# Nine halved token blocks instead of four plain ones and eight halved ones, in an order that the planner chooses itself

## The chip, the cores and the metric

The kernel runs on one core of a Trainium2 chip. The metric is the device time of one execution in microseconds (us); lower is better. Two runs of the kernel before took 1121.74 and 1127.53 us, a median of 1124.63 us.

## The reference

```python
# attention: q, k, v are (8, 8, 576, 64), omega is (128, 64)
scale = 1.0 / np.sqrt(np.sqrt(D)); q_s, k_s = q * scale, k * scale
def phi(x):
    h = np.einsum('bhsd,md->bhsm', x, omega) - np.sum(x * x, -1, keepdims=True) / 2.0
    return np.exp(h - np.max(h, axis=-1, keepdims=True)) / np.sqrt(m)
q_p, k_p = phi(q_s), phi(k_s)
kv = np.einsum('bhsm,bhsd->bhmd', k_p, v); z = np.sum(k_p, axis=2)
attn = np.einsum('bhsm,bhmd->bhsd', q_p, kv) / (np.einsum('bhsm,bhm->bhs', q_p, z)[..., None] + 1e-06)
x = attn.transpose(0, 2, 1, 3).reshape(8, 576, 512)
# Fourier mixing, normalisation, two dense layers
mixed = np.real(np.fft.fft(np.fft.fft(x, axis=1), axis=2))
u = x + mixed
un = (u - mean(u)) / np.sqrt(var(u) + 1e-06)            # over the last axis
out = u + np.maximum(un @ w_ch1, 0.0) @ w_ch2           # w_ch1 (512, 2048), w_ch2 (2048, 512)
```

All matrix work is done in float32. The two weight matrices arrive as float64 and are narrowed to float32 on the chip.

## The kernel before

The 8 x 576 = 4608 rows pass through two parts.

**The first part** holds the attention, the Fourier mixing and the preparation of the weights. `attn` runs 32 times, once for each pair of heads: transposes on TensorE (PE, L607), projections (L701), a row maximum on VectorE (DVE, L644), exponentials on ScalarE (ACT, L661), the products with v and with the features (L735, L782, L790), and a division (L799 to L811). Four pairs make one batch, and `mix` runs once for each of the 8 batches: `folds` adds and subtracts halves on DVE or GpSimd (POOL) (L838 to L874), PE multiplies with sine and cosine tables (L894, L904, L944, and L955 for the middle column), and `residual` joins the cosine part, the sine part and the middle column on DVE (L993, L996) and adds the result to x (L1005, L1006). The sums u go to the tensor `us` in DRAM. `narrow` turns each 512-column piece of the float64 weights into float32 (L532 to L550), first w1, then w2; `w2_parts` makes the sums of w2 that the second part needs (L1484) and stores them in `w2l`.

**The dense layers** work on tokens in two ways. Plain rows are multiplied as they stand: `plain_of` takes 128 rows at a time, with 64 first-layer products (L1236), 16 second-layer products 512 columns wide (L1259), a relu between them (`hidden`, L1220 and L1222) and `rest`. Halved blocks of 512 rows use Strassen's scheme in Winograd's form: one layer of a block is 7 outer products of half-size matrices instead of 8 (`first_of` for the first layer, `product_of` for the second), and most outer products are split again into 7 "leaves" of 4 small products each (`leaf`: L1727 first layer, L2178 second layer). An outer product that is not split again runs at L1878; `single(j)` names those. Before the change the first 512 rows are plain (`NPLAIN = 4`), and the other 4096 rows are 8 halved blocks: block 0 with six of its seven first-layer products unsplit, block 1 alone ("narrow", 128-column leaves), and blocks 2 to 7 in three pairs ("wide", first-layer leaves 256 columns wide; `WIDE = 2`). The plain rows are multiplied in the first part, between the attention's own products; the halved blocks make up the second part. The attention's PE work, the plain rows and the second part follow one another on the same PE queue.

**The order.** Every stream of work (a generator) yields `Step`s with an engine, an expected cost, events to wait for, and buffers and PSUM banks to take and give back. `Listing.run` merges the streams into one in-order list per engine. Left to itself it takes at each turn the step that can begin first by its own clock (`FIRST`, `SECOND`), and of those within a small slack the one with the earliest due time. Where a step may run on DVE or POOL, it takes the one that would finish first. Before the change this choice is overridden: the strings `PICKS` and `PICKS2` name the stream and the engine of each step, `BANKS` and `BANKS2` the PSUM bank, and `BETWEEN` and `BETWEEN2` the places at which the norms of blocks 1 to 3 (`ahead`, L1596 to L1610) are slipped in, in buffers borrowed from the attention.

**Names that the steps below touch.** `w1_sums` makes the outer sums of w1 (`so5`, `so6`, `so3`) that the outer products 5, 6 and 3 multiply with; `sums_right` makes the token sums `tt`; `wl` are the tiles into which the 49 second-layer leaves of w2 are loaded for each narrow block or pair; `tag_of` says which buffer such a tile takes; `wash` are a few short matmuls at the seam of the two parts.

Of the kernel before, what the change touches and what calls it, by code (L numbers as in the profile page):

```python
# [33 lines left out]
NL = 2  # L34
# [7 lines left out]
class Clock(NamedTuple):  # L42
# [23 lines left out]


PICKS = (
    "40e0fff03eafdaege3OcdceefdcOdeccfgda37ghj0gjj7hlP79aj7ik97i8S7efhjffeHldffiehdjfdOihgihidaKedbhhciff"
    "ecgOfeejdfdPdeeedgifdffdefd8aiii88jhd8jP8b99i8e8jcddghjgheiifcOcdciieicgPgdefJcdghbkededfgcRbggb79ij"  # L70
    "8hi7hjafN9Haj9gfffeg8eif8hcej1jccc7ehidbhffLigebfbe6766gggfcbjahj9Ofghhjj8dQkkgT6jghff8de6dUjfhbgegh"
    "cefhafjUf8jgciSjOckkhjakkaeikggjlioklnhSgodoXON7l7l6nnj9icadc97cibf98ejH88a7edhMlhkmjjaQVijihkkfplSm"
    "okliljjilVaghVhnmljkmpjkhhnmkimlgglmbjpjjQ9d9alafhhdjlaMdjback0j766k7lh4g896ck6gkki77gij5ijhgj6dimni"
    "3ndjgi6Kc4jldlKikbkaijLhf75dcjlmklk36ci45jciekajkkkk5kihokeaeoLaioNlencidonbSiljjcmjjkboijTUUhgcfkik"
    "hiflkmeFF99nol5m8jT7naabda89Rbj97ecdl8cjilOgifkQb4acahg57ebbgabgdjkdTkk6eceebb5f9dg4R6ce486ggg6egfhh"
    "fg4g9egf5cbdhgPRhhcgjhggejigibLmHnbedijj6NOb7biihi9bgihMkaffPa8cijdhbdghbaeibNefffacjicigifi99975ih5"
    "jgj8699ajfg6g7fgefd65bO6Kalkkgd5jgjikagfldliPJpeoaeeefgdejadgilgScljiii5e65k56kl57k7j67S9lilk9gliih6"
    "ffkgec4fg4dbgg7fedaiP5gfbheefilddddddeghg9kbfncgghcfkkafkagGngb65p5Hopoj4bhoanbelli68bjjl5b7dlhighhi"
    "lflhpkgiWomjknmmmkimnjbjhn9jkmFKkfFgedccff6Wf7idUVhi8Th3fogbqp8fgmkeSdjna7ckenoghmnmffnjeo79q6547oa4"
    "nlkpd7aceonnc8blSVicilbhmjim8fh7SnnIl5mUkfjgfhhfhihg8ghfbS4kjf83j4lllb79jei8mnkblfnmmiolpilOUi9Mh5l5"  # L80
    "pmnaem79jjVmkbblek5iji9a9kffTgjikhiShfgjafhgfigh4g50PPP0ba5Pdh9dghdK77hgfdcbg8OO988jMehefibjjkellfcc"
    "PcdhQMihfQcffbKCf82b3c98cbcdcd6a299efgddbJaGQQbefLa9ecf74gg986HRgf9idg8kQeheff7be6ff2e5cc8fbcgdKP8f8"
    "9hN9Lc999bddcHcNb7Oc9effegd7ibhQeQ8haf7ccghhlUikhHW5lWmm5dkMQGM71fS6d1gdb99747ifddhIfdhhdhfdbihgiljn"
    "gWgijgg93ekKl8kEhIIbT3jjKgkb9k9eTfhkhlje34m49974iG66h68faHe6e7a79982975aI94a39c8cM8b4aa7ab984fge8eLM"
    "98b86ce8PbFPc9cbe6cKPf3a9b94fIdIQeJKbd876eJPdc5fNb7ffbf9JSS8RiLa4a7gPbajfgg8gdfhg2i2787Hf6OcdIN5d3LH"
    "accd46ddeKK72dJc7bbaa4bb9a9bc7c0777dghhdf7Bfddebd76ff1fddIe9949438686bc6aca85348dHcG7a5be957b55d1544"
    "9Gc1F5a9a68446344584584E59189970955888574443113301110"
)

BANKS = (  # L90
    "0102346120164024306243643016204164024320632462014021604606245062345042604670426420340267407231640260"
    "4524016460620240674206206415704602546064320143607264506402346234062732017426042106147026740260462462"
    "0410652604632452017205467402624060404256174302642060245016745202642016420634520520650162505605260250"
    "1675602501605204672016204567627450264102316742067460260462045642062637230724672402630145420640106240"
    "5264023026731602454230412046450416725730620424670121726154305610207453"
)

PLACES = "kkktttkktuuu"  # L100


BETWEEN = (
    "1684016841169001690116950169501695016950171011710117101175011750217502175031762417625176361766317664"
    "1769217692176931769417712177121776317774177751785317853179041790417926180471804818055180551806618066"
    "1814518145182071820718207182081820818208182261822618377183881846718468"
)


BETWEEN2 = (  # L110
    "006390119901259015590198902149023690236a0262a0265a0301a0329a0355a0426a0486b0528b0528b0550b0552b0563b"
    "0578b"
)

PICKS2 = (
    "020022020000018019023022023020020024021020025024019125125023025023023023028044023022020017018042042043"
    "026040041018018018018035120041034040035034120041043042048023032046030045045037044037046019120120040031"
    "040119019031022036038030032032024045145045145049033122047036034039017047033042042048023046037045025036"
    "043027042019024141143042119045038036048032049033022025050050039036039041043048031034044043022028049044"
    "023054033018032040039053047048027031018039037053038028052053036050040043040048054049038053053036047020"  # L120
    "046037048044117126039023032043042037024044026035044037043032051024025054019046046038119033053047052044"
    "035028044048028041049047047147019044042046044119046044046044048050040053031038025037038039033025052019"
    "046038047135041035029150048034131148033044044050147053028040025144142043147030046047021045043047029042"
    "029053045039052046045051029038038052050026037050049050046046049047051049041044151040040048043050049032"
# [1509 lines left out]

# [754 lines left out]
```

## Time and profile before

| what | value |
|---|---|
| two runs, median | 1121.74 and 1127.53, 1124.63 us |
| span of the profiled execution (first to last instruction) | 1119.2 us |
| PE busy | 1108.4 us (99%) |
| DVE busy | 888.7 us (79%) |
| ACT busy | 539.5 us (48%) |
| POOL busy | 390.6 us (35%) |
| mean granted TensorE clock | 0.999 |
| last plain product begins (L1259) | 416.5 us |
| last row maximum of the attention begins (L644) | 355.3 us |

The profile is of one execution, for which the span is given and no time of its own; the span lies 2.5 us below the faster of the two timed runs and 5.4 us below their median. A float32 product appears in the trace as two PE instructions. The windows view gives for each stretch of the span the busy time of each engine, with the number of instructions in brackets, the granted clock (1.00 is full), the share of the DMA engines and GB/s.

### The profile page before, as it was taken

The numbers are of one execution on the slowest core, as the hardware profiler recorded it, in microseconds if no ns is written. First come the engines' busy times: TensorE is split into PE (matmuls) and PEld (weight loads), VectorE is DVE, ScalarE is ACT, GpSimd is POOL, SyncE is SP. The second block draws the span as 40 slices with busy tenths as digits, with TensorE's granted clock in tenths as the row PEclk, the third lists the DMA queues.
The fourth block names the chain that finished last, engine by engine and source line by source line (L and its number), as shares of the span: only waits on it lengthen the run. The fifth ranks groups of instructions, "written<-read, shape, count | busy, mean of one in ns | idle before, by whom it ended". The sixth has DMA issues, their size and how long they took to land.

```text
span 1119.2 us, 31666 instructions
## 1 busy us (share of the span) xinstructions
PE 1108.4 (99%) x12467; PEld 1000.4 (89%) x12467; DVE 888.7 (79%) x1685; ACT 539.5 (48%) x1644; POOL 390.6 (35%) x401
## 2 busy tenths in 40 slices
PE   9999999999999999999999999999999999999998
PEld 7888888879868778999999889999889999889998
DVE  6999999987576767687697777888677888568895
ACT  7998898856536455623214452223463223331221
POOL 2443443553563348634413464000365000152000
PEclk9999999999999999999999999999999999999999
DMA  8856766665674669798896778747678656546453
GB/s 243 243 174 188 242 180 191 183 208 176 216 232 156 194 172 343 224 314 262 260 326 224 226 216 248 207 148 238 206 207 261 207 155 216 170 152 220 146 160 105
DMA packets 196549, 236.13 MB, mean 211 GB/s; under 512 B 53808, under 2 KB 120624, under 8 KB 196400
## 3 DMA queue, kind: packets, MB, share of 16 engines
q1 hardware_dynamic: 195904, 233.83, 68.1%
q8 instruction: 99, 1.62, 0.6%
q14 instruction: 50, 0.41, 0.1%
q10 hardware_dynamic: 496, 0.26, 0.1%
HBM read 182.13 MB, written 56.10 MB: 213 GB/s over the span
## 4 chain that ended last, share of the span: by engine, by line
PE 92%; DVE 3%; ACT 2%; DMA 2%; issue 0%; POOL 0%; SPq 0%; DVEq 0%; ACTq 0%
PE banks L2178 31%; PE banks L1727 27%; PE banks L1236 5%; PE banks L701 5%; PE banks L607 5%; PE banks L1259 5%; PE banks L1878 4%; PE banks L735 3%; PE banks L782 2%; PE banks L944 2%; PE banks L894 1%; ACT e L661 1%; DVE nmx L644 1%; PE banks L904 1%; DMA unw<-turned 1%; DMA raw<-in_moe_w_ch_dram 1%
## 5 line engine op out<-in xcount | busy, mean ns | idle before, releaser
L2178 PE MATMUL banks<-wl,sums 128*128 128x128 f32 x1792 | 219.8, 275 | 0.0
L2178 PEld LDWEIGHTS banks<-wl,sums 128*128 128x128 f32 x1792 | 210.6, 192 | 1.0 <-issue 0.3
L661 ACT ACTIVATE e<-banks,nmx 128x128 f32<-128x128 f32 x576 | 165.7, 441 | 23.3 <-DVE nmx L644 22.9
L644 DVE TENSOR_REDUCE nmx<-banks 128x8 f32<-128x1024 f32 (+1 forms) x96 | 89.3, 951 | 16.8 <-PE banks L701 12.4
L2178 PE MATMUL banks<-wl,hid 128*128 128x128 f32 x768 | 99.2, 275 | 0.3 <-DVE part L2154 0.3
L2178 PEld LDWEIGHTS banks<-wl,hid 128*128 128x128 f32 x768 | 92.8, 192 | 1.2 <-DVE part L2154 0.8
L2149 ACT ACTIVATE s<-banks 128x128 f32<-128x128 f32 x112 | 30.9, 277 | 113.6 <-PE banks L2178 103.5
L1727 PE MATMUL banks<-unw,wxw 128*128 128x256 f32 x352 | 85.4, 379 | 0.0
L701 PE MATMUL banks<-om,kqT 64*64 64x128 f32 (+1 forms) x2088 | 79.0, 275 | 1.7 <-ACT kv L751 1.3
L701 PEld LDWEIGHTS banks<-om,kqT 64*64 64x64 f32 (+1 forms) x2088 | 64.5, 138 | 12.7 <-issue 3.2
L2178 PE MATMUL banks<-wl,hx 128*128 128x128 f32 x576 | 74.2, 275 | 0.4 <-DVE part L2154 0.4
L1727 PEld LDWEIGHTS banks<-unw,wxw 128*128 128x128 f32 x352 | 66.6, 190 | 8.9
L1727 PE MATMUL banks<-rx,wxw 128*128 128x256 f32 x288 | 70.8, 379 | 0.0
L2178 PEld LDWEIGHTS banks<-wl,hx 128*128 128x128 f32 x576 | 69.4, 192 | 0.8 <-DVE part L2154 0.6
L1752 ACT ACTIVATE s<-banks 128x512 f32<-128x512 f32 x65 | 38.5, 596 | 65.1 <-PE banks L1727 60.0
L1727 PE MATMUL banks<-ttw,wxw 128*128 128x256 f32 x288 | 69.8, 379 | 0.0
L1236 PE MATMUL banks<-unT,w 128*128 128x128 f32 x512 | 65.4, 279 | 1.7 <-DVE qeT L621 1.7
L550 POOL TENSOR_TENSOR w<-w,raw 128x512 f32<-128x512 f32 x28 | 37.6, 1351 | 77.3 <-DVE raw L544 68.1
L2227 POOL TENSOR_TENSOR more<-more,part 128x512 f32<-128x512 f32 x2 | 2.6, 1315 | 176.6 <-ACT part L2220 176.6
L1236 PEld LDWEIGHTS banks<-unT,w 128*128 128x128 f32 x512 | 60.2, 192 | 4.5 <-issue 2.3
L1727 PEld LDWEIGHTS banks<-rx,wxw 128*128 128x128 f32 x288 | 54.5, 190 | 7.3
L1727 PEld LDWEIGHTS banks<-ttw,wxw 128*128 128x128 f32 x288 | 54.5, 190 | 7.3
(287 smaller groups left out, 2442.3 us busy)
## 6 DMA issues: line engine op xcount, KB each, us to landing
wl<-w2l SPq DMA_DIRECT2D x245, 256.0 KB, 3.9
wxw<-w1x SPq DMA_DIRECT2D x120, 256.0 KB, 3.1
raw<-in_moe_w_ch_dram SPq DMA_DIRECT2D x32, 512.0 KB, 4.8
kq<-in_k_dram SPq DMA_DIRECT2D x32, 288.0 KB, 4.5
kq<-in_q_dram SPq DMA_DIRECT2D x32, 288.0 KB, 4.5
vd<-in_v_dram SPq DMA_DIRECT2D x32, 288.0 KB, 5.4
ur<-us SPq DMA_DIRECT2D x30, 256.0 KB, 5.2
w2l<-sums SPq DMA_DIRECT2D x14, 512.0 KB, 4.9
```

Of the source, the lines that this page charges most:

```text
L550: eng.tensor_tensor(out=dst, in0=dst, in1=lof, op=ALU.add)
L607: nc.tensor.transpose(ps[:, (j - j0) * 128 : (j - j0 + 1) * 128], src(j), ident[:])
L644: nc.vector.tensor_reduce(nmx[:, :, 0:num], pps[:, :, 0 : MF * num].rearrange("p b (c m) -> p b c m", m=MF), axis=AX.X, op=ALU.max, negate ...
L661: nc.scalar.activation(out=e[:, c + (i if num == 1 else 0), :], in_=pps[:, i, MF * c : MF * c + MF], func=AF.Exp, bias=nmx[:, i, c : c + 1],)
L701: nc.tensor.matmul(pps[cols, c, MF * m : MF * m + MF], lhsT=kqT[rows, j, cols], rhs=om2[rows, :],)
L735: nc.tensor.matmul(kvp[cols, i, 0 : D + 1], lhsT=feature(r)[rows, cols], rhs=vds[n % NV][rows, r, :], start=(r == 0), stop=(r == R - 1),)
L1236: nc.tensor.matmul(hp[:, 0:TP], lhsT=w1[:, dc, 128 * fc : 128 * fc + 128], rhs=unTs[key][:, dc, :], start=(dc == 0), stop=(dc == NDC - 1),)
L1259: nc.tensor.matmul(yp[:, 0:DM], lhsT=hs[fc][:, 128 * i : 128 * i + 128], rhs=w2[:, fc, :], start=(fc == 0), stop=(fc == NFC - 1),)
L1727: nc.tensor.matmul(ps[:, span * f : span * f + span].rearrange("f (b q) -> f b q", q=Q), lhsT=left[:, P * f : P * f + P], rhs=right, start ...
L1752: nc.scalar.activation(out=s[:], in_=ps, func=AF.Copy)
L1878: nc.tensor.matmul(cell.rearrange("f t (b q) -> f t b q", q=Q), lhsT=w[:, d, col : col + 128], rhs=right[:, :, d].rearrange("f (t b) q -> ...
L2178: nc.tensor.matmul(ps[:, 0:128], lhsT=left[:, f], rhs=wls[head(j), i, n][:, f], start=start and f == 0, stop=(f == 3), skip_group_check=True,)
```

## The change

- `NPLAIN` becomes 0: no row is plain, `plain`, `plain_of`, `plain_norms` and `rest` go, and there are 9 halved blocks. `WIDE` becomes 3: blocks 0, 1 and 2 are narrow, and 3 to 8 make three pairs.
- All seven first-layer products of block 0 are unsplit (`single`), and the first two, 1 and 2, which need no sums, run in the first part (`first_products`, due time 300). Product 2 is not seeded through PSUM but joined on DVE with `relu_sum`, for which `hid` takes the memory of w2 once `w2_parts` is done.
- In `residual` the middle column enters as the bias of an ACT copy for two of the three row groups, and DVE joins with one instruction per sign in place of three.
- w2 is narrowed before w1, and `w2_parts` starts when w2 is there; the raw parts of w1 are stored by `raw_stores`.
- `PICKS`, `BANKS`, `BETWEEN` and their second sets go: `Listing.run` orders both parts itself. The norms of blocks 1 to 3 are no longer slipped into the first part; `late_turns` makes them in the second.
- All `wl` tiles take one of the 12 `wl` buffers; before, 3 of 15 in a narrow block took the buffers `turn` and `u`.

```diff
-    NPLAIN = 4
+    NPLAIN = 0
...
-    w2 = fix.tile([128, NFC, DM], F32, name="w2")
+    w2 = hids.tile([128, NFC, DM], F32, name="w2", tag="hid")
...
         parts = [
-            (w1[:, j, f : f + CV], w1v[:, j, f : f + CV]) for f in range(0, DFF, CV) for j in range(NDC)
-        ] + [(w2[:, j, :], w2v[:, j, :]) for j in range(NFC)]
+            (w2[:, j, :], w2v[:, j, :]) for j in range(NFC)
+        ] + [(w1[:, j, f : f + CV], w1v[:, j, f : f + CV]) for f in range(0, DFF, CV) for j in range(NDC)]
...
+        if c < NL:
+            yield Step(ACT, 0.62, take=("bmp",), bias=0.1)
+            bmp, (aa, mi, pl) = taken()
+            nc.scalar.activation(out=mi[:, KD:], in_=pb[:, KD : KD + 1], func=AF.Copy)
+            nc.scalar.activation(out=pl[:, KD:], in_=pb[:, KD : KD + 1], func=AF.Copy, scale=-1.0)
+            nc.scalar.activation(out=aa[:, 1:KD:2], in_=pa[:, 1:KD:2], func=AF.Copy)
+            for k, mid in ((0, mi), (2, pl)):
+                nc.scalar.activation(out=aa[:, k:KD:4], in_=pa[:, k:KD:4], func=AF.Identity, bias=mid[:, KD:])
+            for last, (dst, op) in enumerate(((mi, ALU.subtract), (pl, ALU.add))):
+                yield Step(DVE, 0.34, give=(b0, b1) if last else (), bias=-0.1)
+                nc.vector.tensor_tensor(out=dst[:, 0:KD], in0=aa[:, 0:KD], in1=pb[:, 0:KD], op=op)
...
-    WIDE = 2
+    WIDE = 3
...
-        return () if j else ORDER0[1:]
+        return () if j else ORDER0
...
+    def block_norms_0():
+        yield Step(NONE, take=("slab",) * 2, after=events_of(range(TB // 128)) + ("converted",))
...
+        yield Step(NONE, take=("slab",) * 2, after=("w2 done",))
...
-        yield Step(NONE, take=("slab",) * 4, after=("converted",))
-        big = [slabs.tile([128, 2, 4, 128], F32, name="big", tag="slab") for _ in range(2)]
+        yield Step(NONE, take=("slab",) * 2, after=tuple(("w", i) for i in range(NFC)))
+        big = [mlpp.tile([128, 2, 4, 128], F32, name="big", tag=f"big{f}", bufs=1) for f in range(2)]
...
-            unseeded = (0,) if not j and i == ORDER0[1] else ()
+            unseeded = range(4) if i == 2 else ()
...
-        n = (49 * j + 7 * order(j).index(i) + PARTS.index(l)) % 15
-        if wide(j) or n % 5 != 4:
-            return "wl", NWL
-        return ("turn", 1) if n == 14 else ("u", 2)
+        return "wl", NWL
...
+    def first_products():
+        yield Step(NONE, after=("w2 done",))
+        spares["hid"] = hids.tile([128, 4, 2, 2, 4 * P], F32, name="hid", tag="hid")
+        for i in ORDER0[:2]:
+            yield Step(NONE, take=("set",))
+            yield Fork(first_of(0, i, 0), 300.0)
+
+    listing.run(
+        [first(), loads(), loads_v(), load_tables(), frames(), mixing()]
+        + [pairs(i) for i in range(NS)]
+        + [w2_parts(), block_norms(0, mlpp), weights(), warm(), raw_stores(), (300.0, first_products())],
+    )
...
-        for j in range(4, NTB):
+        for j in range(1, NTB):
             yield from normed(j, late)
 
     listing.run(
-        [wash(), late_turns(), late_norms(), halves(), load_leaves(), token_sums(0), w1_sums(), w1_inner(), w1_stored()],
-        picked(PICKS2, 3),
-        BANKS2,
-        betweens(BETWEEN2),
+        [wash(), late_turns(), late_norms(), halves(), load_leaves(), w1_sums(), w1_inner(), w1_stored(), (LEAF * 40, weight_sums())],
     )
```

More of the change, by code (lines that the diff above doesn't have):

```diff
@@ L1512, in w2_parts @@
                 )
[L1513 removed]
+        yield Step(NONE, after=last, give=("slab",) * 2, makes="w2 done")
     def sums_left(a11, a12, a21, a22, s1, s2, s4):
@@ L2300, in washed @@
             )
-        yield Step(NONE, give=(b,))
+        yield Step(NONE, after=("held",), give=(b,))
     def halves():
```

346 lines of the change are left out of this document (75 added, 271 removed).

## The prediction

> **What bounds the kernel now.** I read the page first, then the windows, then groups and single lines.
>
> ```profile
> span 1119.2 us, 31666 instructions
> PE 1108.4 (99%) x12467; PEld 1000.4 (89%) x12467; DVE 888.7 (79%) x1685; ACT 539.5 (48%) x1644; POOL 390.6 (35%) x401
> ...
> PE 92%; DVE 3%; ACT 2%; DMA 2%; issue 0%; POOL 0%; SPq 0%; DVEq 0%; ACTq 0%
> ```
>
> PE is busy from end to end, and the chain that ended last is PE for 92%. If that held after the change, only PE's products would count. The windows (columns: stretch, length, then busy us and instructions of PE, PEld, DVE, ACT, POOL, then clock, DMA share, GB/s) say why it may not hold:
>
> ```profile
> 0.00:40.00 40.00, 38.22 (x687) 32.50 (x688) 31.14 (x55) 31.97 (x114) 14.48 (x19) 1.00 0.91 253
> ...
> 40.00:240.00 200.00, 197.01 (x4287) 168.36 (x4286) 189.17 (x422) 171.25 (x610) 85.58 (x86) 1.00 0.64 193
> ...
> 0.00:430.00 430.00, 423.52 (x7597) 351.34 (x7598) 354.68 (x773) 305.44 (x1061) 194.44 (x213) 1.00 0.67 203
> 480.00:520.00 40.00, 40.00 (x360) 40.00 (x359) 33.43 (x63) 11.84 (x36) 14.71 (x13) 1.00 0.96 300
> 800.00:840.00 40.00, 40.00 (x187) 35.22 (x186) 27.69 (x42) 23.13 (x45) 24.41 (x29) 1.00 0.68 198
> ```
>
> From 40 to 240 us DVE is busy for 189.2 of 200 us, 94.6%: it is as full as PE. It slackens only later, where PE is held up by the plain rows. Up to 430 us, where `so6` is ready and block 0's products 5 and 6 can run, DVE has worked 354.7 us. The last two lines give PE's rates: 360 leaf instructions of 128 columns in 40 us are 111.1 ns each, 187 of 256 columns 213.9 ns each.
>
> **The sum for PE.** Gone are the plain products:
>
> ```profile
> L1236 PE MATMUL banks<-unT,w 128*128 128x128 f32 x512 | 65.4, 279 | 1.7 <-DVE qeT L621 1.7
> ...
> L1259 PE MATMUL banks<-w,ht 128*128 128x512 f32 x128 | 58.8, 598 | 0.0
> ```
>
> 512 at 111.1 ns are 56.9 us; the last 32 of L1259 fill 13.7 us in the chain (403.8 to 417.5), so 128 are 54.9: together 111.8 us. Half of the 4.9 us of L1172's transposes goes too. A ninth block, narrow, adds 2 x 392 instructions at 111.1 ns, 87.1 us. Product 1 of block 0 unsplit costs 32 x 213.9 ns = 6.8 us in place of 56 x 111.1 ns = 6.2. Net -26.5 us: by PE alone, 1092.7 us.
>
> But the two sides lie in different parts. The plain rows leave the first part; of the new work only products 1 and 2 (13.7 us) enter it. PE's first part shrinks from 417.5 us to 417.5 - 111.8 - 2.4 + 13.7 = 317 us at most. The second part holds 5 unsplit products (160 x 213.9 ns = 34.2), 9 second layers (3528 x 111.1 = 392.0), two narrow first layers (784 x 111.1 = 87.1) and three wide ones (1176 x 213.9 = 251.5): 764.8 us. The same sum for before is 690.8 us, and the stretch from 417.5 us to the last leaf at 1115.3 took 697.8, 1.0% more. With that, 772.5 us. 3.9 us come behind the last leaf.
>
> **The sum for DVE, up to `so6`.** The changed program's list has 695 DVE instructions up to there, the old one 774. Priced by the rows (busy over count): evictions L621 67 to 16, -17.4 us; `residual`, 144 instructions for 38.3 us, now 32 joins, and 48 as before for the third row group (12.8), -12.1; half of block norms L1162 to L1168, -6.9; L1608, nine slipped-in transposes, -6.3; plain relu and rest (L1220, L1272), -8.1; smaller ones (L749, L550, L811, L838, L1358, L1770), -9.8. Against that the order without `PICKS` gives DVE what POOL did: all 44 w2 sums instead of 10, 34 x 0.69 = +23.4; 30 instead of 13 each of L1005 and L1006, 34 x 0.50 = +17.0; folds L854, L867, L874, +11.8; four `relu_sum` of product 2, +2.8; four more sums of w1, +2.7. Net -2.9, and 79 fewer instructions lose 79 x 0.05 us of overlap (in 0 to 422 us the groups add up to 386.5, the engine was busy for 349.2, 768 instructions): about 355 us. **DVE's work ahead of the second part stays 355 us, while PE's falls to 317.**
>
> The join on 257 columns, one input in PSUM, is not in the trace: between 0.278 us (L996, 128 columns) and 0.69 (L1770, 512 columns), I take 0.42 by width, 13.4 us for 32 (8.9 to 22). The L1005 price lies between these:
>
> ```profile
> L1005 DVE TENSOR_TENSOR x<-x,bmp x13: 407/416/1418, 103.8 to 408.9; 128x257 f32<-128x257 f32 x11, 64x257 f32<-64x257 f32 x2
> ...
> L1683 DVE TENSOR_TENSOR rx<-so x1: 1644/1644/1644, 430.2 to 430.2; 128x512 f32<-128x512 f32 x1
> ```
>
> 0.416 at the median, 0.50 on the mean, as some ran at 1.4; the same width of 512 took 0.69 us alone and 1.64 at 430 us, where POOL was busy for 8.45 of 9 us. With the median DVE has 3 us less. So 347 to 364 us in all. The Trainium skill (SBUF — State Buffer, Who interferes with whom) has a DVE instruction with two SBUF inputs and a GpSimd one that reads SBUF block each other; by that rule, and the trace agrees, POOL's fall from 194 to about 95 us spares DVE those 3 us and the total comes out 3 us lower.
>
> ACT gets 16 x (5 x 0.30 - 0.39) = +18 us for the bias form and some 20 us of evictions, and loses 12.6 (L1222) and 20 (norms of blocks 1 to 3): about 305 us again, under DVE. Weights and norms that change places cost PE nothing themselves; their DVE instructions are counted. The norms of blocks 1 to 3 and a ninth block raise DVE's share of the second part from 77% (534 of 689 us) to some 84% (115 us more), covered by PE. Their DMAs, and 12 `wl` buffers for 15, are a rival below: SP's list grows by 51 issues, 49 of them `wl` and 28 for the norms that come late, less 12 that were slipped in and the rows of the plain blocks; the nine raw stores of w1 now go out in one row behind the last weight, where the leaves that read them are two blocks away. Products 1 and 2 overwrite w2 in memory, so they wait for the last store of `w2_parts` (4.9 us to landing); its sums stand 66 places before `so5` on DVE, some 40 us, which hides it, and without that cover it would cost the 4.9.
>
> **When the second part starts.** In the order of DVE's list `so5` and `so6` stand behind all mixing, all w2 sums and seven inner sums of w1; PE's list has nothing left to do before them but products 1 and 2. With 31.1 us done in the first 40 us, and then 94.6%: 40 + 323.9 / 0.946 = 382 us. In the last batch DVE waits for PE's and ACT's part of the mix (PE: L894, L904 4.2 us, L944, L955 5.2 us per batch) with little else to do; I allow 4. Start 386 us, 31 us earlier than before, with 74 us more behind it.
>
> 386 + 772.5 + 3.9 = 1162 us of span, against 1119.2. The median lay 5.4 us above its span: **1168 us**, 3.8% slower. Own range 1150 to 1182: DVE's 347 to 364 us, at 93% to 97%.
>
> **Rivals.**
> 1. *DVE's queue stalls more in the unaided order.* An instruction that waits holds all behind it, above all the row maxima that ACT's exponentials wait for (22.9 us now). The first 100 us have 88.0 us of DVE work without any plain rows in between. At that pace 355 us take 403: 1185 us; at the first window's 78%, 455: 1237. Against it: with fewer products ahead of it PE answers sooner.
> 2. *DVE runs on without a wait*, since PE and ACT have room: start at 355 us, 1137 us, no change beyond what a measurement can tell (2% is about its limit). Against: a first product cannot come before 3.8 us (L588), and the last batch has its chain.
> 3. *The other side: PE stays fed.* If DVE's list were shorter by a tenth (319 us, more overlap, POOL's blocking gone), PE would decide at 317 us: 317 + 772.5 + 3.9 + 5.4 = 1099 us, 2.3% faster. For it: PE is busy for 38 of 40 us from the start, before any plain row. Against: the same windows have DVE at 94%; it decides only below 320 us of DVE work. The reverse point is the forecast's.
> 4. *DMA bounds the narrow blocks.* 49 leaves of 256 KB in 43.6 us are 295 GB/s; at 480 us the share is 0.96 with 300 GB/s, and there will be three such stages with 12 buffers, a lead of 10.7 us over 3.9 us of landing. At the 264 GB/s of 520 to 560 us each stage lasts 5 us more: 1183 us.
> 5. *The clock falls in the first part.* PE will idle some 70 us there. The rows show 1.00 in every window, the first with 1.8 us of idle time included, and 0.96 only at the end. At half clock throughout, 317 us of products would take 634: 1416 us; up to 69 us more PE time would hide behind DVE. TensorE: Matmul & The Clock Gate, What's actually happening, of the Trainium skill has the clock halve after an idle window of about 3.4 us; no run here shows such an idle spell.
>
> That the change does not do what it says I leave out: the built lists show no L1236 or L1259 and 49 leaves more.
>
> **How the numbers follow.** Forecast 0.58; rival 1 0.17, 2 0.10, 3 0.04, 4 0.08, 5 0.03. Faster by over 2% is rival 3, 0.04; within 2% (1102 to 1147) rival 2, 0.10; slower the rest, 0.86. The range runs from rival 2 to past the lower end of rival 1: 1137 to 1205.
>
> **What would show it.** Right: DVE above 93% between 40 and 350 us and PE below 85%; the first unsplit product on `so5` (L1878) near 386 us, after a wait of PE for DVE; PE at 100% from there, about 772 us; POOL near 95 us in the first part. Wrong: that product before 365 us or after 405, waits of PE for `wl` above 10 us in the narrow blocks, or a clock below 1.00 in the first part.

## The result and the profile after

The changed kernel takes 1219.59 us (two runs, 1219.09 and 1220.09) where the kernel before takes 1124.63: ratio 1.085, 95% interval 1.078 to 1.093. The forecast was 1168 us, with a range of 1137 to 1205. The direction was right; the time lies 52 us above the forecast and 15 us above the range.

First the page of the changed kernel (span, busy time of each engine, share of the chain that ended last by engine):

```profile
span 1217.3 us, 32303 instructions
PE 1121.6 (92%) x12571; PEld 1034.9 (85%) x12571; DVE 974.1 (80%) x1788; ACT 582.1 (48%) x1795; POOL 276.5 (23%) x292
...
PE 76%; DVE 9%; ACT 8%; DMA 5%; issue 1%; SPq 0%; POOL 0%; DVEq 0%; ACTq 0%
```

PE is no longer busy from end to end: 96 us of the span it is idle. Of the chain, 24% now run through other engines and DMAs; before it was 8%. The windows tell where (columns as in the prediction):

```profile
0.00:40.00 40.00, 35.82 (x605) 30.81 (x605) 27.26 (x47) 29.37 (x103) 12.31 (x18) 1.00 0.93 266
40.00:280.00 240.00, 199.88 (x4525) 172.58 (x4528) 224.07 (x428) 190.08 (x712) 70.57 (x53) 0.94 0.60 178
280.00:421.20 141.20, 105.04 (x1802) 88.24 (x1796) 106.55 (x220) 74.73 (x279) 15.50 (x16) 0.87 0.55 176
0.00:421.20 421.20, 340.75 (x6923) 291.63 (x6924) 357.88 (x693) 294.18 (x1091) 98.38 (x86) 0.92 0.61 185
421.20:1217.30 796.10, 780.83 (x5648) 743.29 (x5648) 616.27 (x1096) 287.88 (x704) 178.10 (x206) 0.99 0.73 223
```

The first product on `so5`, the forecast's mark for the second part, begins at 421.2 us, not at 386. The work ahead of it is what the prediction had counted: 357.9 us of DVE (355 forecast), 294.2 of ACT (305), 98.4 of POOL (95). From 40 to 280 us DVE is full, 93.4%. From there on it is not: 106.6 of 141.2 us, 75%. More than half of the 34.7 us in which it does nothing lie ahead of the last row maximum (L556), which begins at 366.5 us; the stretch behind it is

```profile
366.50:421.20 54.70, 40.94 (x450) 33.48 (x445) 40.52 (x90) 18.25 (x69) 3.23 (x4) 0.87 0.38 117
```

with 14.2 us of idle time. The other 20.5 us come between 280 and 366.5 us, where DVE waits for ACT's bias copies (6.8 us, once), for ACT's exponentials (8.3) and for PE. The kernel before shows the same sag in that stretch, under a PE at 99%:

```profile
280.00:420.00 140.00, 138.29 (x1742) 107.42 (x1735) 95.85 (x232) 70.56 (x231) 65.29 (x83) 1.00 0.61 194
```

The timeline of the changed kernel's DVE shows what the end of the first part is made of (start, duration, instruction; in square brackets the idle time before it and what ended it).

```profile
377.54 0.17 DVE L711 TENSOR_SCALAR rden<-banks 128x10 f32<-128x10 f32 x1 [3.72 <-PE banks L702]
...
383.60 1.21 DVE L750 TENSOR_TENSOR half<-x 128x1024 f32<-128x1024 f32 x1
...
396.42 0.17 DVE L786 COPY fold<-half 128x3 f32<-128x3 f32 x1
...
405.63 0.76 DVE L913 TENSOR_TENSOR bmp<-bmp,banks 128x257 f32<-128x257 f32 x2 [5.25 <-ACT bmp L910]
...
411.77 0.41 DVE L933 TENSOR_TENSOR x<-x,bmp 64x255 f32<-64x255 f32 x1
415.14 0.69 DVE L1457 TENSOR_TENSOR rx<-w 128x512 f32<-128x512 f32 x1 [2.96 <-DMA us<-x]
```

It is one chain: exponentials, division (377.5), the folds of batch 7 (383.6 to 396.6), cosine and sine products, bias copies, the join (405.6), the last addition to x (411.8), the store of x, in whose memory `rx` and `so` are laid out (415.1), the sums of w1, and then PE:

```profile
421.23 9.07 PE L1658 MATMUL banks<-tt,so 128*128 128x256 f32 x29 [9.29 <-DVE so L1457]
```

From the last row maximum to this product 54.7 us pass. PE's share of the chain is not the mix alone. Between the cosine and the sine products of the last batch, pieces of products 1 and 2 stand in PE's queue, and the chain that ended last runs through them for 9.0 us:

```profile
392.38 7.17 PE L1658 MATMUL banks<-unT,w 128*128 128x256 f32 x32
...
401.31 1.99 PE L1658 MATMUL banks<-unT,w 128*128 128x256 f32 x8
```

The kernel before has that chain too: its last row maximum begins at 355.3 us, its last addition to x (L1005) at 408.9. There the last plain product began at 416.5 us; now only products 1 and 2 are left beside it.

The second part takes 796.1 us, where 776.4 were forecast (772.5 and 3.9 of tail). Waits of PE in the second part (total, times, longest):

```profile
PE banks L1658 <- DVE so L1457: 9.3, 1, 9.3
PE banks L1954 <- DMA wl<-w2l: 8.8, 4, 4.5
```

The first line is the wait ahead of 421.2 us. Nearly all the others are for `wl` leaves, at 486 us and from 661 to 670 us, and the granted clock falls behind them.

### The profile page after: what moved, and what is told of

Read it like the earlier page. It is cut to its first block, busy times and chain, and to the rows that moved or that the text cites. A ratio compares the mean times of both kernels' runs of the same rounds, so it can differ in the third digit from the quotient of the medians.

```text
span 1217.3 us, 32303 instructions
## 1 busy us (share of the span) xinstructions
PE 1121.6 (92%) x12571; PEld 1034.9 (85%) x12571; DVE 974.1 (80%) x1788; ACT 582.1 (48%) x1795; POOL 276.5 (23%) x292
## 4 chain that ended last, share of the span: by engine, by line
PE 76%; DVE 9%; ACT 8%; DMA 5%; issue 1%; SPq 0%; POOL 0%; DVEq 0%; ACTq 0%
PE banks L1954 31%; PE banks L1501 26%; ACT e L573 5%; PE banks L1658 4%; PE banks L613 4%; PE banks L647 3%; PE banks L519 3%; PE banks L694 2%; PE banks L806 2%; DVE nmx L556 2%; DMA wl<-w2l 2%; PE banks L816 1%; DMA raw<-in_moe_w_ch_dram 1%; DVE x L933 1%; ACT qeT L535 1%
## 5 line engine op out<-in xcount | busy, mean ns | idle before, releaser
L1954 PE MATMUL banks<-wl,sums 128*128 128x128 f32 x2016 | 250.4, 278 | 0.7 <-DMA wl<-w2l 0.5
L1954 PEld LDWEIGHTS banks<-wl,sums 128*128 128x128 f32 x2016 | 240.4, 195 | 1.6 <-issue 1.0
L573 ACT ACTIVATE e<-banks,nmx 128x128 f32<-128x128 f32 x576 | 159.3, 443 | 32.7 <-DVE nmx L556 32.7
L1954 PE MATMUL banks<-wl,hid 128*128 128x128 f32 x936 | 122.0, 278 | 8.7 <-DMA wl<-w2l 8.3
L1954 PEld LDWEIGHTS banks<-wl,hid 128*128 128x128 f32 x936 | 113.8, 194 | 9.9 <-issue 4.7
L613 PE MATMUL banks<-om,kqT 64*64 64x128 f32 (+1 forms) x2088 | 91.0, 295 | 29.9 <-ACT e L573 23.7
L613 PEld LDWEIGHTS banks<-om,kqT 64*64 64x64 f32 (+1 forms) x2088 | 75.7, 151 | 41.6 <-ACT e L573 29.3
L556 DVE TENSOR_REDUCE nmx<-banks 128x8 f32<-128x1024 f32 (+1 forms) x96 | 87.3, 951 | 20.4 <-PE banks L613 12.9
L1925 ACT ACTIVATE s<-banks 128x128 f32<-128x128 f32 x126 | 34.9, 277 | 132.9 <-PE banks L1954 116.4
L1930 DVE TENSOR_TENSOR part<-banks,s 128x128 f32<-128x128 f32 x114 | 33.0, 290 | 49.6 <-PE banks L1954 44.4
L519 PE MATMUL banks<-ident,kq 128*128 128x128 f32 x288 | 44.8, 296 | 17.0 <-ACT e L573 10.9
L1970 ACT ACTIVATE banks<-banks 128x128 f32<-128x128 f32 x63 | 16.6, 263 | 86.3 <-PE banks L1954 83.9
```

The costliest lines, as they stand in the source:

```text
L519: nc.tensor.transpose(ps[:, (j - j0) * 128 : (j - j0 + 1) * 128], src(j), ident[:])
L556: nc.vector.tensor_reduce(nmx[:, :, 0:num], pps[:, :, 0 : MF * num].rearrange("p b (c m) -> p b c m", m=MF), axis=AX.X, op=ALU.max, negate ...
L573: nc.scalar.activation(out=e[:, c + (i if num == 1 else 0), :], in_=pps[:, i, MF * c : MF * c + MF], func=AF.Exp, bias=nmx[:, i, c : c + 1],)
L613: nc.tensor.matmul(pps[cols, c, MF * m : MF * m + MF], lhsT=kqT[rows, j, cols], rhs=om2[rows, :],)
L1925: nc.scalar.activation(out=s[:], in_=ps[:, 0:128], func=AF.Copy)
L1930: nc.vector.tensor_tensor(out=part[:, t, 128 * m : 128 * m + 128], in0=ps[:, 0:128], in1=saved[with_][:], op=ALU.add,)
```

## The experiments

All ratios are to the kernel before, run on the same chip with it. A profile is of one execution. Five kernels below have the instruction lists of the changed kernel up to its last row maximum, and it comes at 367.1 us (half_leaves), 370.3 (products_last), 370.7 (tags_as_before), 371.5 (warm_seam) and 372.7 (thin_products) in place of 366.5. So a start of the second part that differs by 6 us in two traces need not come from the edit.

### The old structure in the planner's own order

```diff
-        picked(PICKS, 1),
-        BANKS,
-        betweens(BETWEEN),
...
-        for j in range(4, NTB):
+        for j in range(1, NTB):
...
-        picked(PICKS2, 3),
-        BANKS2,
-        betweens(BETWEEN2),
```

> The kernel before (four plain blocks, eight halved ones), but with its order left to the planner as in the changed kernel, and with the norms of blocks 1 to 3 late. Theory (the plain rows kept PE fed while DVE worked off the first part's list): PE over 95% busy in the first part, 1130 to 1155 us in all. Rival (the unaided order itself costs most of the 95 us): PE below 90% there, 1185 us or more.

Measured: 1221.17 us, ratio 1.087 (1.085 to 1.089). The rival holds, the theory falls: four plain and eight halved blocks lose all 97 us by the order and the late norms alone, and are then as slow as the nine blocks. Products on `so5` begin at 498.4 us, 71 us later than before (427.7). The windows show a part of it:

```profile
240.00:320.00 80.00, 79.08 (x823) 60.13 (x826) 39.34 (x87) 26.07 (x93) 3.78 (x6) 1.00 0.63 209
320.00:440.00 120.00, 101.94 (x2387) 88.97 (x2377) 95.37 (x209) 88.14 (x324) 18.08 (x20) 0.96 0.44 133
```

The plain rows run in a heap from 240 to 320 us, with PE full and DVE half idle, and then the attention runs alone, with PE at 85%. In the written order the two lie in each other's gaps. But the loss begins earlier. Up to 240 us PE has about as much plain work as before (156 instructions of L1236 and L1259, 147 before), and yet it is idle for 34.1 us, 4.8 before. So the plain rows alone do not keep PE fed; the order counts.

### The written order in the first part alone

```diff
-        betweens(BETWEEN),
...
-        for j in range(4, NTB):
+        for j in range(1, NTB):
...
-        picked(PICKS2, 3),
-        BANKS2,
-        betweens(BETWEEN2),
```

> The kernel before with its written order and banks kept in the first part alone; the second part is ordered by the planner itself and all norms of the halved blocks come in the second part, as in order_only. Theory: both parts lose by the unaided order, and independently; order_only began block 0's products on so5 71 us later than before (498.4 against 427.6 us) and took 30 us more behind that, so this kernel has only the second loss: products on so5 at 427 +- 5 us, median 1152 us (1140 to 1165). Rival: the second part's loss follows from the way the first part ends (late norms and weight sums pile up there), so with the old first part the rest runs at the old pace: median 1122 to 1133 us.

Measured: 1152.77 us, ratio 1.026 (1.023 to 1.029), products on `so5` at 428.1 us. The theory's figure to the microsecond: of the old structure's 97 us, 68 are the order of the first part, 29 belong to the second. What the 29 are is the next question. Waits of PE in this kernel:

```profile
PE banks L2177 <- DMA wl<-w2l: 19.3, 7, 13.4
```

### Late norms, or the order of the second part

norms_early puts the norms of blocks 1 to 3 back to their old places and leaves only order and banks of the second part to the planner; picks_first_12 keeps the late norms and takes every `wl` leaf into the 12 `wl` buffers, as the changed kernel does.

```diff
 norms_early, against before:
-        picked(PICKS2, 3),
-        BANKS2,
+        (),
+        "",
         betweens(BETWEEN2),
 picks_first_12, against picks_first:
-        n = (49 * j + 7 * order(j).index(i) + PARTS.index(l)) % 15
-        if wide(j) or n % 5 != 4:
-            return "wl", NWL
-        return ("turn", 1) if n == 14 else ("u", 2)
+        return "wl", NWL
```

> picks_first, but with the norms of the halved blocks 1 to 3 slipped in at their written places as before, ahead of the blocks that need them; only the order and banks of the second part are the planner's own. Theory: the 29 us that picks_first lost in its second part come from the late norms (their loads and stores in SP's queue, and their hold on the buffers turn and u, which the wl leaves borrow), so this kernel is back at the time of before: median 1122 to 1131 us. Rival: the planner's own order of the second part costs them, whenever the norms are made: median 1145 to 1155 us.

> picks_first (late norms), but with all wl leaves in the 12 wl buffers as in the changed kernel, none in turn and u. Theory: of the 19.3 us that PE waited for wl in picks_first, the 13.4 us of the longest wait and the clock that falls behind it come from leaves that wait for a borrowed buffer held by a late norm; with 12 buffers they go and the shorter waits stay: median 1134 to 1142 us. Rival: the leaves are late because of their place in SP's queue behind the stores of the norms, whatever their buffer: median 1148 to 1156 us.

Measured: norms_early 1123.29 us, ratio 0.999 (0.998 to 1.001); picks_first_12 1138.39 us, ratio 1.013 (1.011 to 1.015). Both theories hold. The written order and banks of the second part are worth nothing that these runs can tell (the norms keep their written places in norms_early); all 29 us come from norms that are made there. Half of that is the borrowed buffers: with 12 `wl` buffers the waits of PE for `wl` fall from 19.3 to 6.5 us.

### The leaves of w2 in the changed kernel

half_leaves loads half of each leaf of the narrow blocks and uses it twice, which leaves half of their second-layer weights out of the computation; tags_as_before lends them the buffers `turn` and `u` again, 15 in all.

```diff
 half_leaves:
-                    nc.sync.dma_start(wl[:].rearrange("p f m -> p (f m)"), w2l[i][STORED.index(l)])
+                    if wide(j):
+                        nc.sync.dma_start(wl[:].rearrange("p f m -> p (f m)"), w2l[i][STORED.index(l)])
+                    else:
+                        nc.sync.dma_start(wl[:, 0:2].rearrange("p f m -> p (f m)"), w2l[i][STORED.index(l)][:, 0:256])
...
-    rhs=wls[head(j), i, n][:, f],
+    rhs=wls[head(j), i, n][:, f if wide(j) else f % 2],
```

> The changed kernel, where the narrow blocks load half of each wl leaf (128 KB for 256 KB) and use that half twice; half of the second-layer weights of blocks 0 to 2 is left out of the computation. Theory: the 20 us that the second part lost against its forecast come from wl leaves that land late in the narrow blocks (13 us of waits of PE) and from the clock that falls behind those waits (some 5 us): without them the second part takes 778 to 783 us in place of 796, median 1201 to 1206 us. Rival: the leaves are late because of where their issues stand in SP's queue, not because of their bytes: the waits stay, median 1215 to 1222 us.

> The changed kernel with 15 buffers for the wl leaves of narrow blocks as before (three of 15 in the buffers of turn and u) in place of 12. Theory: the lead of the loads, 12 leaves of 0.89 us, is what is short: with 15 the waits of PE for wl (13 us) halve at least, median 1208 to 1214 us. Rival: the lead is not the limit, or the leaves then wait for the late norms that hold the borrowed buffers: median 1216 to 1230 us.

Measured: half_leaves 1207.89 us, ratio 1.075 (1.072 to 1.079); its second part takes 781.7 us by the windows:

```profile
421.90:1203.60 781.70, 774.57 (x5648) 737.64 (x5648) 616.92 (x1096) 287.27 (x704) 178.68 (x206) 1.00 0.66 203
```

14.4 us less than 796.1, as the theory has it, with the clock back at 1.00 and PE's 774.6 us close to the 772.5 forecast. The median fell by 11.7, just short of the expected range. tags_as_before takes 1233.67 us, ratio 1.097 (1.094 to 1.101): the rival. More buffers make it slower. One line of its PE timeline, and one of SP's waits between 560 and 680 us:

```profile
652.57 2.04 PE L1957 MATMUL banks<-wl,sums 128*128 128x128 f32 x8 [10.86 <-DMA wl<-w2l]
```

```profile
SPq L1018 <- DVE turn L1012: 10.3, 5, 3.5
```

From 617 to 649 us SP issues no leaf; it works at the norms' loads and stores and waits for their transposes. That a leaf needs a buffer which a late norm still holds, as the rival says, fits this and the pair picks_first and picks_first_12; this run does not separate it from the leaves' place in SP's list.

### Norms of blocks 1 and 2 in the tail of the changed kernel

```diff
+    def early_norm(j, i):
+        buf = ("kq", "turned")[i % 2]
+        yield Step(SP, 0.42, 3.0, take=(buf,), ..., after=events_of(...) + (("kq", B * NP - 1),))
+        ...                       # mean, variance, scaling and transpose as in ahead
+        yield Step(SP, 0.55, 6.0, makes=("turned", j, i), give=(buf,), kb=165)
...
+        + [(310.0 + j, early_norm(j, i)) for j in (1,) for i in range(TB // 128)],      # (1, 2) in norms_tail_12
...
-        for j in range(1, NTB):
+        for j in range(2, NTB):      # 3 in norms_tail_12
```

> The changed kernel, where the four norms of block 1 are made in the tail of the first part (in buffers of the attention, once the last keys are loaded) and not in the second part. Theory: the late norms are what makes wl leaves late; the wait of 4.5 us at 486 us and the clock behind it go with block 1's norms, the waits at 661 to 670 us stay, and the tail has room for four norms (2.8 us of DVE, 8 of ACT, 4 of POOL): products on so5 at 419 to 424 us, second part 787 to 790 us in place of 796, median 1209 to 1214 us. Rival: the second part is bound by the wl loads themselves, so the waits stay: 794 to 798 us, median 1217 to 1224 us.

> As norms_tail_1, with the eight norms of blocks 1 and 2 in the tail. Theory: two thirds of the late norms are gone, so both the wait at 486 us and part of those at 661 to 670 us go: second part 780 to 786 us. If the tail's idle time takes all eight (5.5 us of DVE, 15 of ACT), products on so5 stay at 419 to 424 us and the median is 1202 to 1210 us. Rival: eight norms stand between the steps of the last batch on ACT and DVE and move products on so5 to 428 us or later, so that the gain is given back: median 1212 to 1222 us.

Measured: norms_tail_1 1216.9 us (1213.5 to 1222.9), ratio 1.083 (1.079 to 1.087): no gain that the runs can tell. The trace, of the fastest of its four runs, tells more: products on `so5` at 423.5 us, second part 788.2 us, 7.9 less than 796.1, as expected. Its idle spells of PE behind 424 us:

```profile
653.83 1.13 PE L1954 MATMUL banks<-wl,sums 128*128 128x128 f32 x8 [0.15 <-DMA wl<-w2l]
661.40 1.64 PE L1954 MATMUL banks<-wl,hid 128*128 128x128 f32 x8 [3.74 <-DMA wl<-w2l]
671.61 1.55 PE L1954 MATMUL banks<-wl,hid 128*128 128x128 f32 x8 [2.07 <-DMA wl<-w2l]
```

The wait at 486 us is gone with block 1's norms, those of 661 to 670 us stay. norms_tail_12 takes 1237.35 us, ratio 1.100 (1.097 to 1.103), its rival and worse: products on `so5` at 451.2 us, the last row maximum at 410.0. Eight norms don't fit into the tail: in DVE's list five of their transposes stand ahead of the last row maxima, and DVE waits 10.6 us for ACT at these transposes. Its second part, 789.2 us, is no shorter than with four, so block 2's norms aren't what the waits near 661 us hang on. What else is (the norms of the wide blocks come there) was not tried.

### What the first part is bound by

Four kernels change the work in it: the sums of w2 on POOL; no sums of w2, with zeros stored in their place; the old three joins; and products 1 and 2 left out, with a few short bf16 products in their place.

```diff
 sums_on_pool:
-            eng = nc.gpsimd if step.eng == POOL else nc.vector
-            eng.tensor_tensor(out=o, in0=l, in1=r, op=ALU.subtract)
+            nc.gpsimd.tensor_tensor(out=o, in0=l, in1=r, op=ALU.subtract)
 no_w2_sums:
-            step = Step({DVE: 0.6, POOL: 1.24}, port=True, **kw, bias=-0.63)
...
+            yield Step(NONE, **kw)
 three_joins:
-            nc.scalar.activation(out=aa[:, k:KD:4], in_=pa[:, k:KD:4], func=AF.Identity, bias=mid[:, KD:])
...
-                nc.vector.tensor_tensor(out=dst[:, 0:KD], in0=aa[:, 0:KD], in1=pb[:, 0:KD], op=op)
+                nc.vector.scalar_tensor_tensor(...)      # twice, and a third join of the odd columns
 thin_products:
+                    thin = not j and i in ORDER0[:2]
+                    for h in range(2 * thin):
+                        nc.tensor.matmul(ps[:, 256 * h : 256 * h + 256], lhsT=eye[:, 0:128], rhs=eye, ...)
-                    for n in range(2):
+                    for n in range(2 * (not thin)):
```

> The changed kernel with all 44 sums of w2 put on POOL in place of DVE, nothing else moved in the order. Theory (DVE's amount of work sets the start of the second part): DVE loses 28 us, the first product on so5 comes 25 us earlier, near 396 us, 1192 to 1200 us in all. Rival (the chain through the last batches sets it, whatever DVE's amount): the start within 8 us of 421, 1211 to 1222 us.

> The changed kernel without the 44 sums of w2 on DVE (30.4 us of its work, all between 264 and 374 us); zeros are stored in place of the sums, and the sums are left out of the computation. Theory: what DVE does there stands in one chain with the last two batches, so most of it comes back: products on so5 at 393 to 403 us in place of 421, median 1191 to 1202 us. Rival: the last batches are bound by the answers that DVE, ACT and PE give each other and by free PSUM banks, and the sums lie in the gaps: products on so5 at 414 to 421 us, median 1212 to 1220 us.

> The changed kernel with the old form of residual for the first two row groups (one ACT copy, three DVE instructions per sign), steps and order unchanged. Theory (DVE sets the pace of the first part): DVE gets 12 us more, ACT 13 us less, start 10 to 13 us later, 1228 to 1234 us. Rival (ACT sets it): start up to 10 us earlier, 1208 to 1217 us.

> The changed kernel, where products 1 and 2 of block 0 are replaced by two short bf16 matmuls for each of their eight PSUM banks; 13.7 us of PE work in the tail of the first part become about 1.8, and the two products are left out of the computation. Evictions and sums on DVE and ACT stay. Theory: from the last row maximum on, the last batch runs through one chain (division, folds, cosine and sine products, bias copies, joins, store, sums of w1) of some 50 us in which PE has room, so 12 us less of PE work move little: products on so5 at 416 to 421 us, median 1213 to 1220 us. Rival: the pieces of products 1 and 2 stand ahead of the last batch's matmuls in PE's queue and stretch the chain by most of their length: products on so5 at 408 to 413 us, median 1206 to 1212 us.

Work of DVE and POOL is what the windows give up to the first product on `so5`.

| kernel | last row maximum at | products on `so5` at | DVE, POOL until then | median us | ratio (interval) |
|---|---|---|---|---|---|
| changed kernel | 366.5 | 421.2 | 357.9, 98.4 | 1219.59 | 1.085 (1.078 to 1.093) |
| sums_on_pool | 376.4 | 432.7 | 346.7, 155.4 | 1230.03 | 1.096 (1.094 to 1.098) |
| no_w2_sums | 361.1 | 419.3 | 334.9, 95.8 | 1213.39 | 1.079 (1.074 to 1.085) |
| three_joins | 376.1 | 431.3 | 364.9, 98.6 | 1228.92 | 1.095 (1.091 to 1.098) |
| thin_products | 372.7 | 422.1 | 356.8, 98.7 | 1219.76 | 1.086 (1.084 to 1.089) |

In no_w2_sums, without the 30 us of sums, DVE is simply idle where they stood:

```profile
320.00:360.00 40.00, 32.47 (x785) 28.18 (x787) 22.69 (x45) 32.00 (x118) 2.35 (x1) 0.91 0.80 268
360.00:400.00 40.00, 34.01 (x383) 28.20 (x374) 24.35 (x56) 13.68 (x53) 1.32 (x2) 0.88 0.15 44
```

With 23 us less on DVE the start moves by 1.9 us and the median falls by 6.2, both in the rival's ranges. But this does not show that DVE's work counts for nothing, because the planner's order moved as well. The last row maximum comes 5.4 us earlier. Then products 1 and 2 stand in one piece in PE's queue, from 370.9 to 384.9 us, ahead of the products that the last division waits for, and that division comes at 386.2 us, where the changed kernel has it at 378.7. From 366 to 424 us the clock is 0.71, where the changed kernel has 0.87 from 366.5 us on:

```profile
366.00:424.00 58.00, 40.77 (x362) 33.55 (x359) 37.13 (x83) 11.80 (x42) 5.82 (x5) 0.71 0.35 104
```

thin_products doesn't begin earlier either, though it leaves out 12 us of PE work. But its last row maximum came 6.2 us later under the same list, and from there to `so5` 49.3 us pass. In the changed kernel it is 54.7, and 52.1 to 56.1 in half_leaves, tags_as_before and warm_seam, where the two products stand as in the changed kernel. So in the tail they cost some 3 to 7 us.

The sums on POOL start the second part 11.5 us later. On POOL one takes 1.26 to 1.67 us, on DVE most take 0.68; which step of the chain waits for them, this run doesn't separate. DVE has only 11 us less to do, although 30 us of sums are gone: with POOL busier, other instructions of DVE took 19 us more, the additions to x above all. Their means are 599 and 787 ns here, 427 and 609 in the changed kernel:

```profile
L933 DVE TENSOR_TENSOR x<-x,bmp 128x255 f32<-128x255 f32 (+1 forms) x30 | 23.6, 787 | 0.0
...
L932 DVE TENSOR_TENSOR x<-x,bmp 128x257 f32<-128x257 f32 (+1 forms) x30 | 18.0, 599 | 0.0
```

So this run is no test of a lighter DVE. three_joins, where the extra work lies in the stretch in which DVE is full, starts 10.1 us later. By the windows DVE has 7.0 us more to do, not 12; already the last row maximum comes 9.6 us later (376.1). That is what the bias form is worth here, and up to 6 us of it can be the spread between executions.

Together: the tail is a chain through ACT, DVE, PE and SP; neither DVE's amount of work alone nor PE's sets its length, and PE's order has a part in it. How much each engine contributes, these runs don't separate.

products_last holds products 1 and 2 until the last mix is done.

```diff
-        yield Step(NONE, after=("w2 done",))
+        yield Step(NONE, after=("w2 done", "mixed"))
```

> The changed kernel with products 1 and 2 of block 0 held back until the last batch's mix has its products behind it. Theory (they stand between the halves of the last mix and delay it by some 9 us, and then PE idles 9 us before so5): start of the products on so5 8 to 10 us earlier, 1207 to 1212 us. Rival (they fill time that is free): no gain, or up to 14 us later, 1218 to 1233 us.

Measured: 1218.9 us, ratio 1.086 (1.083 to 1.089), products on `so5` at 423.7 us: no gain, the rival. One wait took the place of another: product 2's `relu_sum` now stands ahead of the sums for `so5` in DVE's queue and waits for PE until 422.3 us.

### The clock at the seam

```diff
+        if i == len(CLEAN) - 1:
+            for _ in range(36):
+                nc.tensor.matmul(ps[:, 0:128], lhsT=zeros[:], rhs=zeros[:], start=True, stop=True, ...)
```

> The changed kernel with 72 more PE instructions (36 products of zeros) behind the wash, so that PE isn't idle while it waits for so5 (9.3 us). Theory: the clock of 0.55 in the 6 us behind that wait is the consequence of the idle time; with PE busy the first products on so5 run at full clock (379 ns each from the first one on, not up to 764) and the second part begins 2.6 us earlier: median 1215 to 1218 us, window 421 to 427 us at a clock of 0.95 or more. Rival: the clock there follows from something else (the whole first part at 0.92), and stays under 0.8: median 1218 to 1222 us.

Measured: 1226.8 us, ratio 1.093 (1.089 to 1.096). The zeros go into the last washed bank, so what accumulates there begins from another state. As a time this run decides nothing: its first part, the same list, ran 5 us later already at the last row maximum (371.5 us against 366.5). Nor was the seam closed: the zeros end at 425.1 us and the first product comes at 427.6, after 2.6 us without work, and the clock fell behind these too. How it fell is told below.

## Why the prediction was right and wrong

**PE's sum was right.** The first part holds 340.8 us of PE time at a mean clock of 0.92, some 320 at full clock (317 forecast at most). The second part's 772.5 us are 774.6 in half_leaves, where nothing waits for a leaf.

**DVE's list was right**: 357.9 us against 355; that POOL would hand its share to DVE, and ACT's 294, came as counted.

**When the second part starts: wrong by 35 us.** 386 came from 31.1 us of work by 40 us, a pace of 94.6% to the end of the list, and "I allow 4" for the last batch.
- By 280 us DVE had done 251.3 us of work where that pace gives 258.1; the first window alone holds 27.3 for 31.1. At 94.6%, 7.2 us.
- The list was 2.9 us longer: 3.1 us.
- From 280 us on, 106.6 us of work took 141.2. At the old pace they take 112.6, with the allowance 116.6. The other 24.6 us are the step that failed: **the pace of 94.6% was carried on to the end of the list, with 4 us for the last batch's chain.** Ahead of the last row maximum 66.0 us of work took 86.5 (69.8 at the old pace), 16.7 us lost, while DVE waited for ACT and PE. Behind it 40.5 us took 54.7 (42.8 at the old pace, 46.8 with the allowance), 7.9 us lost.

The prediction read DVE's slack behind 240 us as "PE is held up by the plain rows". In the changed kernel, without any plain rows, the slack is still there. The row maximum at 355.3 us and the last addition to x at 408.9 us stood in the trace of before. In the 53.6 us between them plain products (160 instructions of L1236 and 45 of L1259, some 37 us at their rates) filled most of PE's time, and the change takes them out. That their absence is the whole cause is not shown. order_only keeps the plain rows and still begins block 0's products on `so5` 71 us late, so that the planner's order costs time with them too. How the 24.6 us are shared between the order and the missing rows stays open.

**Norms in the second part "covered by PE": wrong.** They cost no PE time, but their loads and stores share SP's queue and the DMA engines with the leaves. The second part is 19.7 us longer than 776.4, of which some 11 us are idle time of PE and 8 us clock, 2.6 of these at the seam. On the structure of before, the same move costs 15 us with 12 `wl` buffers and 29 with 15 (norms_early, picks_first_12, picks_first); taking block 1's four norms out of it gives 7.9 us back in one trace of the changed kernel, while the medians show no gain. The 12 buffers, which the prediction had listed as a risk, were a gain: 1233.7 us with 15.

The three terms make 34.9 of the 35.2 us by which the start was missed, and 386 + 35.2 + 776.4 + 19.7 = 1217.3, the span. The median lay 2.3 us above it, not 5.4.

**The rivals.** Rival 1 (the unaided order makes DVE's queue stall) has the right time range, 1185 to 1237, and part of its mechanism is there. ACT's exponentials waited longer for the row maxima, 32.7 us in the changed kernel, 22.9 before:

```profile
L573 ACT ACTIVATE e<-banks,nmx 128x128 f32<-128x128 f32 x576 | 159.3, 443 | 32.7 <-DVE nmx L556 32.7
```

```profile
L661 ACT ACTIVATE e<-banks,nmx 128x128 f32<-128x128 f32 x576 | 165.7, 441 | 23.3 <-DVE nmx L644 22.9
```

Up to 280 us DVE was busy for 89.8% of the time, between the forecast (92.2) and the rival (88.0), and that cost 7 us; that most of the loss would come behind 280 us the rival did not say. Rival 4 (DMAs bound the narrow blocks, 15 us) was sized well: half_leaves gets 14.4 us back. It should have been in the sum. But its cause, bytes alone, is not what the runs show: with early norms the narrow blocks of the old structure lose nothing (norms_early), so that its size is in part luck. Rival 5 came true in part: the clock of the first part is 0.92, some 20 us of PE time; in the second part the clock costs some 8 us. Whether it also moves the start is not shown. In the six traces with the same list the last row maximum came at 366.5 and 367.1 us where the clock from 160 to 200 us was 0.91 and 0.90, and at 370.3 to 372.7 us where it was 0.80 to 0.85. Rivals 2 and 3 fall: DVE does wait, and PE is idle for 80 us of the first part.

**The marks.** DVE was at 88.6% from 40 to 350 us (274.7 of 310), not above 93; PE at 81%, below 85 as said; the product on `so5` behind 405 us and a clock below 1.00 were two of the three signs named as "wrong". The third, waits for `wl` above 10 us, was not reached: PE waited 8.8 us, and the 4.3 us for which its weight loads waited lie in the same gaps.

**Nine blocks or eight?** Under the planner's own order the two structures take the same time: 1219.6 and 1221.2 us. On the old structure the loss is that of the first part's order, 68 us, and of the late norms, 15 to 29 us. That the nine blocks lose by the same two is not shown: what they would take in an order written out for them, with the tail filled, no run here tells.

## What to carry to other kernels

Before taking work off the busiest engine, look for the latency chain that this work covers: follow the last batches from their first instruction to the last store in the old trace and ask what will run beside it. A pace read where an engine is full can't be extended over the end of a pipeline. A step moved to a later part is not free because the engine there has room: count its DMAs in the queue and the buffers it shares with the loads that feed the busiest engine.

## What was not expected of the hardware

The granted clock falls to half behind quite short pauses of PE, and the fall can come late. In the changed kernel PE stops at 411.9 us (windows of two and one us: busy times, then clock, DMA share, GB/s):

```profile
410.00:412.00 2.00, 0.38 (x2) 0.10 (x1) 2.00 (x9) 0.58 (x2) 0.00 (x0) 1.00 0.57 115
412.00:414.00 2.00, 0.00 (x0) 0.00 (x0) 0.17 (x1) 0.58 (x1) 0.00 (x0) 0.70 0.93 289
...
422.00:424.00 2.00, 2.00 (x6) 1.55 (x6) 2.00 (x5) 0.00 (x0) 1.04 (x1) 0.50 0.88 283
...
426.00:428.00 2.00, 2.00 (x10) 1.69 (x9) 1.97 (x2) 0.47 (x1) 0.96 (x1) 0.89 1.01 358
```

By the means of these windows the clock fell at 412.8 us and rose at 426.4: 13.6 us, four times 3.4. Work resumes at 421.2 us and so runs at half clock for 5 us: one fp32 instruction of 256 columns takes up to 764 ns there, 379 at full clock. In warm_seam a pause of 2.55 us was enough, and the clock fell only when PE was at work again (a line of PE's timeline with the pause, then the windows):

```profile
427.62 4.56 PE L1658 MATMUL banks<-tt,so 128*128 128x256 f32 x12 [2.55 <-issue]
```

```profile
427.00:428.00 1.00, 0.38 (x2) 0.30 (x2) 1.00 (x3) 0.00 (x0) 0.00 (x0) 1.00 1.05 361
428.00:429.00 1.00, 1.00 (x5) 0.81 (x4) 1.00 (x3) 0.00 (x0) 0.00 (x0) 0.69 0.94 270
429.00:430.00 1.00, 1.00 (x4) 0.81 (x3) 1.00 (x3) 0.00 (x0) 0.65 (x1) 0.50 1.01 373
...
431.00:432.00 1.00, 1.00 (x4) 0.82 (x3) 1.00 (x3) 0.37 (x1) 1.00 (x1) 0.61 1.03 389
```

There it was at 0.50 from about 428.4 to 431.8 us, 3.4 us. In the 3.4 us ahead of each of the two falls PE had worked for 0.8 and 0.9 us. The Trainium skill (TensorE: Matmul & The Clock Gate, What's actually happening) describes a monitor that judges PE's activity in free-running windows of about 3.4 us and grants half or full rate. The trace agrees with the two rates and the length, and the late fall fits a window that is judged after it has ended. It names at least one idle window as the condition for half rate. Here no window wholly without work was needed: the pause of 2.55 us lay between stretches in which PE was full. The prediction gave a falling clock 0.03, since 1.8 us of idle time in the first 40 us of before had left it at 1.00.
